# A fused attention and feed-forward kernel: another order of the opening on TensorE, and a later slot for one batch's projections

## The chip, the cores and the metric

The kernel runs on one core of a Trainium2 chip. The metric is the device time of one execution in microseconds. Five runs of the kernel before are shown, and one execution was profiled. Names of engines: PE is TensorE (matmuls), PEld its weight loads, DVE is VectorE, ACT is ScalarE, POOL is GpSimd, SP is SyncE. "L411" is line 411 of the kernel.

## What is computed

For 8 batches of 8 heads, with 1024 positions and 64 features per head, keys and values are first projected along the sequence to 64 rows (E and F), then a softmax attention is taken over these 64 rows, and the result goes through a feed-forward pair of matrices with a sigmoid-type GELU:

```python
k_proj = einsum('ks,bhsd->bhkd', E, k)            # 64 rows for each head
v_proj = einsum('ks,bhsd->bhkd', F, v)
scores = q @ k_proj.T / sqrt(64)
attn = softmax(scores)                            # over 64
x = (attn @ v_proj), heads side by side           # 8192 x 512
h = x @ w_in                                      # 8192 x 2048
out = (h * sigmoid(1.702 * h)) @ w_out            # 8192 x 512
```

Inputs and output are 32-bit floats; the kernel works in bfloat16 with 32-bit sums.

## The kernel before, in words

The 8192 tokens are cut into 16 blocks of 512 (two per batch). For each block j, `ffn1` (L405) makes 16 groups of 128 hidden features with four matmuls each, followed by a GELU on ACT; `ffn2` (L415) makes the four output tiles of 128 tokens, each out of 16 matmuls in two parts of eight. All else is put between these: a dictionary `fill` holds, for a block and a slot, the steps that are issued after that slot's matmuls (`at`, L446, and `filled`, L528). Slots 0 to 15 of a block follow one `ffn1` group each, slots O = 16 to 23 one part of `ffn2` each. The order of instructions on each engine is the order in which the program issues them; the tile library adds the waits.

For a batch b, `proj(b)` (L168) projects k and v (16 matmuls), `kv_out(b)` (L223) copies k's result on DVE, transposes it by a DMA from SP's queue into `kts`, and copies v's into `vqs`. `q_dma(b)` (L254) transposes q by a DMA, too. `scores(h, u)` (L274) is the score matmuls of half of the heads of block h, and their exp on ACT. `sums(h)` (L298) sums the exps of all heads in two `x_ps` tiles and takes reciprocals on DVE; `spread(h)` (L313) writes those to DRAM (`rdr`) and reads them back over the partitions (`rbc`), by DMAs from SP's queue. `values(h, u)` (L335) multiplies exps and projected v on PE, and DVE scales the two tiles by `rbc` (L341). Blocks 1 and 2 use `tok` and `x_tr` (L378, L393) for the same. PSUM is two pools of four buffers each: `f_ps` (L40), used by projections, scores, `ffn1` and `ffn2`, and `x_ps` (L41), used by sums, values, the transposes of x and some of the scores.

Loads go through POOL's queue in the order written at L88 to L105: k of batch 0 in three pieces, half of q, v in three pieces, w_in in eight pieces (two groups of hidden features each) with the other half of q among them, w_out in four, then batch 1. The buffers of k, v and q are single (q has two), so that a later load waits for the projection or transpose that reads the batch in them; `load(b)` for b from 2 on is issued at the start of block 2(b - 2).

The opening is block 0, written out by hand at L453 to L481. `k_piece` (L185) projects a piece of k and transposes it on PE. `q_tr0(g, u, cp)` (L234) makes eight transposes of q (half g of the block's tokens, half u of the heads) into an `f_ps` tile and copies it with the engine `cp`. `scores(0, u, half)` then works on 256 tokens. `sums0(half)` (L351) sums exps for 256 tokens with narrow matmuls, `v_piece` (L205) projects a piece of v, `tok0(p)` (L360) makes the values of a pair of heads and scales them on DVE in two instructions, and `x_tr0` (L370) transposes the result into x on PE and copies it. `warm(n)` (L140) is n matmuls on zeros whose result nobody reads. `gelu_table()` loads ACT's table.

Of the kernel before, what the change touches and what calls it, by code (L numbers as in the profile page):

```python
# [10 lines left out]
BF16 = mybir.dt.bfloat16  # L11
# [6 lines left out]
def kernel(ctx, tc, q, k, v, E, F,  # L18
                                                     moe_w_in, moe_w_out, out):
    nc = tc.nc  # L20
# [3 lines left out]
    P = 128  # L24
# [5 lines left out]
    TB = 512  # L30
    JB = TB // P
# [9 lines left out]
    ps_x = ctx.enter_context(tc.tile_pool(name="ps_x", bufs=4, space=PSUM))  # L41
# [50 lines left out]
    ident = consts.tile([P, P], BF16)  # L92
# [9 lines left out]
    for i in range(4):  # L102
        sl = slice(i * FC // 4, (i + 1) * FC // 4)
# [33 lines left out]
    def f_tile(shape, dt=F32):  # L137
        return ps_f.tile(shape, dt, name="f_ps")

    def warm(n, f=False):  # L140
        w_ps = f_tile([P, TB]) if f else ps_x.tile([P, TB], F32, name="x_ps")
        for _ in range(n):
            nc.tensor.matmul(w_ps, zeros[:, :P], zeros, start=True, stop=True)  # L143
# [18 lines left out]
    def eft(j, cols=slice(0, 2 * KP)):  # L162
        return efts[j // (J // 2)][:, j % (J // 2), cols]
# [4 lines left out]
    def proj(b):  # L168
        def go():
            kvps[b] = f_tile([P, H, D])  # L170
            for j in range(J):
                for e, r in enumerate((LO, HI)):
                    nc.tensor.matmul(kvps[b][r], eft(j, slice(e * KP, (e + 1) * KP)),  # L173
                                     (kt, vt)[e][b][:, :, j, :],
                                     start=(j == 0), stop=(j == J - 1))
        return go
# [8 lines left out]
    def k_piece(h0, n):  # L185
        k_ps = proj0(0, h0, n)
        k_b = att.tile([KP, n, D], BF16, name=f"k0_b{h0}", bufs=1)
        nc.vector.tensor_copy(k_b, k_ps[LO])
        warm(2)
        k_tr(k_b, h0 // 2)  # L190
# [14 lines left out]
    def v_piece(h0, n):  # L205

        v_ps = proj0(1, h0, n)
        if n == 4:
            nc.vector.tensor_tensor(vx0[0][:, :, :D], v_ps, mask, op=ALU.mult)
        else:  # L210
            for t in range(n):
                nc.scalar.activation(vx_of(0, h0 // 2)[:, t, :D], v_ps[:, t, :], AF.Identity,
                                     scale=rows[:, h0 % 4 + t:h0 % 4 + t + 1])

    def v_out(b, v_ps):
        vv = v_ps[HI].rearrange("k (u x) d -> k u x d", x=4)
        for r, xs_ in ((LO, X_LO), (HI, X_HI)):
            if b == 1:
                vx = vx1[r, :, :D].rearrange("k (u x) d -> k u x d", x=4)
                nc.vector.tensor_copy(vx[:, :, xs_], vv[:, :, xs_])  # L220
            nc.vector.tensor_copy(vqs[b % 2][r].rearrange("k (u e) d -> k u e d", e=2), vv[:, :, xs_, :])

    def kv_out(b):  # L223
        def go():
            ps = kvps.pop(b)
            k_b = att.tile([KP, H, D], BF16, name="k_b")
            nc.vector.tensor_copy(k_b, ps[LO])  # L227
            nc.sync.dma_start_transpose(out=kts[b % 2], in_=k_b.rearrange("k h d -> k (h d)"))
            v_out(b, ps)
        return go  # L230
# [3 lines left out]
    def q_tr0(g, u, cp):  # L234
        t_ps = f_tile([P, 2, 2, P], BF16)
        for jj in range(2):
            for h in range(4):
                r = h % 2 * D
                nc.tensor.transpose(t_ps[r:r + D, jj, h // 2, :], qt[0][:, 4 * u + h, 2 * g + jj, :], ident)
        cp(q0s[g][u], t_ps)  # L240
# [33 lines left out]
    def scores(h, u, half=None, x=False):  # L274
        b, c = divmod(h, NB2)
        j0, n = (c * JB, JB) if half is None else (c * JB + half * JB // 2, JB // 2)
        ts = slice(j0 * P - c * TB, (j0 + n) * P - c * TB)

        def go():
            if h not in expT:  # L280
                expT[h] = att.tile([P, HP, TB], BF16, name="expT", bufs=3)
            s_ps = [(x_tile() if x else f_tile([P, TB]))[:, :n * P] for _ in range(2)]
            eight(s_ps, [kts[b % 2][:, 2 * u + i, :] for i in range(2)],
                 [q0s[half][u][:, :, i, :] if h == 0 else qT[b][:, j0:j0 + n, 2 * u + i, :]
                   for i in range(2)])
            for i in range(2):
                nc.scalar.activation(expT[h][:, 2 * u + i, ts], s_ps[i], AF.Exp, scale=scale)  # L287
        return go

    def gelu_table():  # L290
        nc.scalar.preload_act_table(AF.Gelu_apprx_sigmoid)  # L291

    def x_of(h):
        if h not in xT:
            xT[h] = att.tile([P, KC, TB], BF16, name="xT", bufs=3)
        return xT[h]

    def sums(h):  # L298


        def go():
            d_ps = [ps_x.tile([P, TB], F32, name="x_ps") for _ in range(2)]
            for p in range(HP):
                for e in range(2):
                    r = HI if (p + e) % 2 else LO
                    nc.tensor.matmul(d_ps[e][32 * p:32 * p + 32], ones[r, :32], expT[h][r, p, :], start=True, stop=True)  # L306
            rden = att.tile([P, 2, TB], F32, name="rden", bufs=1)
            for e in range(2):
                nc.vector.reciprocal(rden[:, e, :], d_ps[e])  # L309
            rdens[h] = rden  # L310
        return go

    def spread(h):  # L313
        def go():
            rdr = dram.tile([HP, 2, TB], F32, name="rdr")
            nc.sync.dma_start(out=rdr, in_=rdens.pop(h)[0:P:32])
            rbc[h] = att.tile([P, HP, TB], F32, name="rbc")
            for e, r in enumerate((LO, HI)):
                nc.sync.dma_start(out=rbc[h][r], in_=rdr[None, :, e, :].to_broadcast([D, HP, TB]))
        return go  # L320
# [25 lines left out]
    xs = {}  # L346
# [4 lines left out]
    def sums0(half):  # L351
        d_ps = ps_x.tile([P, HP, 2, 2], F32, name="x_ps")
        for p in range(HP):
            for i in range(2):
                t = 2 * half + i
                nc.tensor.matmul(d_ps[:, p, i, :], expT[0][:, p, t * P:(t + 1) * P],
                                 vx_of(0, p)[:, :, D:].rearrange("r t o -> r (t o)"), start=True, stop=True)
        nc.vector.reciprocal(rd0[:, half], d_ps)

    def tok0(p):  # L360
        n_ps = ps_x.tile([P, 2, 2, 2, D], F32, name="x_ps")
        for t in range(JB):
            nc.tensor.matmul(n_ps[:, t // 2, t % 2].rearrange("s t d -> s (t d)"),
                             expT[0][:, p, t * P:(t + 1) * P], vx_of(0, p)[:, :, :D], start=True, stop=True)
        xs[p] = work.tile([P, 2, 2, 2, D], BF16, name="x0_sb", bufs=4)
        for a in range(2):
            nc.vector.tensor_tensor(xs[p][:, a], n_ps[:, a], rd0[:, a, p, :, :, None].to_broadcast([P, 2, 2, D]),
                                    op=ALU.mult)

    def x_tr0(p, parts, cp):  # L370
        n_ps = ps_x.tile([P, JB, P], BF16, name="x_ps")
        for g in range(parts):
            for t in range(g * JB // parts, (g + 1) * JB // parts):
                nc.tensor.transpose(n_ps[:, t, :], xs[p][:, t // 2, t % 2].rearrange("s t d -> s (t d)"), ident)  # L374
            sl = slice(g * JB // parts, (g + 1) * JB // parts)
            cp(x_of(0)[:, p, sl.start * P:sl.stop * P], n_ps[:, sl].rearrange("r t s -> r (t s)"))

    def tok(h, p, half):  # L378
        def go():
# [66 lines left out]
    def at(j, slot, *fs):  # L446
        fill.setdefault((j, slot), []).extend(fs)
# [5 lines left out]
    for h0, n in ((0, 4), (4, 2), (6, 2)):  # L453
        k_piece(h0, n)
    DV, AC = nc.vector.tensor_copy, nc.scalar.copy
    for half in range(2):
        q_tr0(half, 0, DV)
        q_tr0(half, 1, AC)
        for u in range(2):
            scores(0, u, half, u > 0)()  # L460
    warm(1)
    sums0(0)
    gelu_table()
    warm(1, True)
    v_piece(0, 4)
    sums0(1)
    v_piece(4, 2)
# [2 lines left out]
    warm(1, True)  # L470
    v_piece(6, 2)
    tok0(2)
    x_tr0(0, 1, AC)
    warm(1, True)
    x_tr0(1, 1, AC)
    tok0(3)
    warm(1, True)
    x_tr0(2, 1, AC)
    warm(1, True)
    x_tr0(3, 2, DV)  # L480
    warm(1, True)  # L481
    at(0, 13, q_tr(2))
    at(0, 15, q_tr(3))
    for u in range(2):
# [15 lines left out]
        at(1, O + 6, scores(3, u, None, u > 0))  # L500
    at(1, O + 6, gelu_table)
    at(1, O + 4, q_dma(2))
    at(2, 1, proj(2), kv_out(2), sums(3), spread(3))
    at(2, O, q_dma(3))
    at(2, O + 3, scores(5, 0))
    at(2, O + 6, proj(3), kv_out(3), scores(5, 1), sums(4), spread(4))
# [25 lines left out]
    for j in range(NBLK):  # L532
# [5 lines left out]
        parts = [(n, range(8 * g, 8 * g + 8)) for n in range(JB) for g in range(2)]  # L538
# [36 lines left out]
```

## Time and profile before

| | us |
|---|---|
| five runs | 510.13, 509.69, 513.47, 512.19, 512.19 |
| median of the runs | 512.19 |
| profiled execution, its own time | 510.13 |
| profiled execution, span from first to last instruction | 508.4 |
| PE busy in it | 499.8 |
| q's transposes begin on PE | 13.76 |
| ffn1 of block 0 begins on PE | 23.14 |
| proj(2) begins on PE | 89.11 |
| sums(4) begins on PE | 119.19 |

Times in the profile count from the first instruction. A row of the timeline has the start, the length, the engine, the line, the operation, what it writes and reads, the shapes, how many instructions of the kind follow one another, and in brackets the idle time of that engine before, with what ended it. Matmuls follow one another before the earlier ones have ended, so a row's length is a little more than the time to the next row's start. A row with SPq or POOL is the issue of a DMA; the data land later.

### The profile page before, as it was taken

The numbers are of one execution on the slowest core, as the hardware profiler recorded it, in microseconds if no ns is written. First come the engines' busy times: TensorE is split into PE (matmuls) and PEld (weight loads), VectorE is DVE, ScalarE is ACT, GpSimd is POOL, SyncE is SP. The second block draws the span as 40 slices with busy tenths as digits, with TensorE's granted clock in tenths as the row PEclk, the third lists the DMA queues.
The fourth block names the chain that finished last, engine by engine and source line by source line (L and its number), as shares of the span: only waits on it lengthen the run. The fifth ranks groups of instructions, "written<-read, shape, count | busy, mean of one in ns | idle before, by whom it ended". The sixth has DMA issues, their size and how long they took to land.

```text
span 508.4 us, 7125 instructions
## 1 busy us (share of the span) xinstructions
PE 499.8 (98%) x3049; PEld 226.9 (45%) x3049; DVE 154.7 (30%) x206; ACT 262.6 (52%) x429; POOL 77.2 (15%) x96
## 2 busy tenths in 40 slices
PE   7899999999999999999999999999999999999997
PEld 3644445444444444444444444444444444444444
DVE  4413204607251624216161330616223161611000
ACT  1665473655637365572746537374563737243351
POOL 7442150510600510051000510000000000000000
PEclk9999999999999999999999999999999999999999
DMA  9999999999899999598939969090703205050202
GB/s 165 200 203 207 215 152 173 202 207 139 159 208 256 118 183 185 159 141 93 221 58 209 122 112 229 26 226 0 173 0 83 86 17 151 0 168 0 84 0 84
DMA packets 124696, 68.77 MB, mean 135 GB/s; under 512 B 90564, under 2 KB 115524, under 8 KB 122744
## 3 DMA queue, kind: packets, MB, share of 16 engines
q0 software_dynamic: 83360, 29.37, 53.9%
q1 hardware_dynamic: 41224, 38.69, 30.6%
q8 instruction: 24, 0.39, 0.3%
q10 hardware_dynamic: 80, 0.26, 0.2%
q14 instruction: 8, 0.07, 0.0%
HBM read 72.88 MB, written 16.99 MB: 177 GB/s over the span
## 4 chain that ended last, share of the span: by engine, by line
PE 96%; DMA 2%; POOL 1%; ACT 1%; issue 0%; DVE 0%; POOLq 0%
PE f_ps L411 44%; PE f_ps L435 43%; PE f_ps L173 3%; DMA q_even<-in_q_dram 2%; PE f_ps L268 2%; PE x_ps L268 1%; PE f_ps L427 1%; PE x_ps L306 1%; POOL k_sb L57 0%; PE x_ps L383 0%; PE f_ps L181 0%; PE x_ps L398 0%; PE f_ps L143 0%; ACT expT L287 0%; PE f_ps L250 0%; PE x_ps L374 0%
## 5 line engine op out<-in xcount | busy, mean ns | idle before, releaser
L435 PE MATMUL f_ps<-w_out_sb,gT 128*128 128x512 bf16 x1008 | 226.7, 379 | 0.0
L411 PE MATMUL f_ps<-xT,w_in_sb 128*128 128x512 bf16 (+1 forms) x1032 | 224.3, 377 | 0.0
L413 ACT ACTIVATE gT<-f_ps 128x512 bf16<-128x512 f32 (+1 forms) x258 | 150.5, 594 | 61.9 <-PE f_ps L411 61.7
L411 PEld LDWEIGHTS <-w_in_sb 128*128 128x128 bf16 x1032 | 100.6, 98 | 119.8 <-issue 0.6
L435 PEld LDWEIGHTS <-gT 128*128 128x128 bf16 x1008 | 95.8, 98 | 121.8 <-issue 11.8
L438 ACT COPY o_sb<-f_ps 128x512 f32<-128x512 f32 x63 | 37.0, 587 | 130.7 <-PE f_ps L435 120.9
L341 DVE TENSOR_TENSOR xT<-x_ps,rbc 128x512 bf16<-128x512 f32 x52 | 33.4, 685 | 219.6 <-PE x_ps L268 117.0
L309 DVE RECIPROCAL rden<-x_ps 128x512 f32<-128x512 f32 x26 | 85.3, 3323 | 9.6 <-PE x_ps L306 9.6
L70 POOL DMA_DIRECT2D q_sb<-in_q_dram x48 | 42.1, 901 | 154.7 <-DMA qT<-q_sb 125.6
L287 ACT ACTIVATE expT<-f_ps 128x512 bf16<-128x512 f32 (+1 forms) x54 | 28.5, 580 | 29.4 <-PE f_ps L268 29.3
L287 ACT ACT_TABLE_LOAD x13 | 16.7, 1283 | 4.7 <-PE f_ps L268 4.5
L291 ACT ACT_TABLE_LOAD x14 | 18.0, 1283 | 0.2
L57 POOL DMA_DIRECT2D k_sb<-in_k_dram x10 | 8.5, 848 | 47.6 <-PE f_ps L173 44.7
L227 DVE CAST k_b<-f_ps 64x512 bf16<-64x512 f32 x7 | 4.8, 681 | 33.2 <-PE f_ps L173 33.2
L173 PE MATMUL f_ps<-k_sb,eft 128*64 128x512 bf16 x56 | 13.4, 382 | 0.0
L173 PE MATMUL f_ps<-v_sb,eft 128*64 128x512 bf16 x56 | 13.4, 382 | 0.0
L429 DVE COPY o_sb<-f_ps 128x256 f32<-128x256 f32 (+1 forms) x2 | 0.7, 358 | 37.3 <-issue 36.9
L268 PE MATMUL x_ps<-expT,vq 64*32 64x512 bf16 x208 | 10.2, 378 | 0.0
L268 PE MATMUL f_ps<-qT,kt 64*32 64x512 bf16 x200 | 10.2, 386 | 0.0
L57 POOL DMA_DIRECT2D v_sb<-in_v_dram x10 | 8.3, 838 | 7.8 <-DMA q_sb<-in_q_dram 4.1
L173 PEld LDWEIGHTS <-eft 128*64 128x64 bf16 x112 | 5.7, 109 | 7.3 <-issue 3.0
L268 PEld LDWEIGHTS <-kt 64*32 64x32 bf16 x272 | 3.6, 89 | 11.8 <-issue 11.1
(75 smaller groups left out, 129.9 us busy)
## 6 DMA issues: line engine op xcount, KB each, us to landing
out_dram<-o_sb SPq DMA_DIRECT2D x15, 1024.0 KB
rbc<-rdr SPq DMA_DIRECT2D x26, 512.0 KB
k_sb<-in_k_dram POOLq DMA_DIRECT2D x7, 1024.0 KB, 13.8
v_sb<-in_v_dram POOLq DMA_DIRECT2D x7, 1024.0 KB, 19.5
q_sb<-in_q_dram POOLq DMA_DIRECT2D x48, 128.0 KB, 7.7
w_in_sb<-in_moe_w_in_dram POOLq DMA_DIRECT2D x8, 256.0 KB, 12.2
w_out_sb<-in_moe_w_out_dram POOLq DMA_DIRECT2D x4, 512.0 KB, 14.8
q_even<-in_q_dram POOLq DMA_DIRECT2D x2, 512.0 KB, 10.7
```

Source lines behind the costliest of these rows:

```text
L57: nc.gpsimd.dma_start(out=dst[b][:, h:h + n, js:js + jn], in_=sv[:, h:h + n, js:js + jn])
L70: nc.gpsimd.dma_start(out=qt[b][:, j], in_=qv[:, j])
L173: nc.tensor.matmul(kvps[b][r], eft(j, slice(e * KP, (e + 1) * KP)), (kt, vt)[e][b][:, :, j, :], start=(j == 0), stop=(j == J - 1))
L268: nc.tensor.matmul(outs[i][r.start + c:r.start + c + 32], lhsTs[i][ri, c:c + 32], rhss[i][ri], start=True, stop=True)
L287: nc.scalar.activation(expT[h][:, 2 * u + i, ts], s_ps[i], AF.Exp, scale=scale)
L291: nc.scalar.preload_act_table(AF.Gelu_apprx_sigmoid)
L309: nc.vector.reciprocal(rden[:, e, :], d_ps[e])
L341: nc.vector.tensor_tensor(x_of(h)[:, 2 * u + i, :], n_ps[i], rbc[h][:, 2 * u + i, :], op=ALU.mult)
L411: nc.tensor.matmul(h_ps, w_in_sb[:, kc, fc * P:(fc + 1) * P], xT[j][:, kc, ts], start=(kc == 0), stop=(kc == KC - 1))
L413: nc.scalar.activation(gts[j][:, fc, ts], h_ps, AF.Gelu_apprx_sigmoid)
L435: nc.tensor.matmul(o_ps[n], gts[j][:, fc, n * P:(n + 1) * P], w_out_sb[:, fc, :], start=(fc == 0), stop=(fc == FC - 1))
L438: nc.scalar.copy(osb[j][:, n, :], o_ps.pop(n))
```

## The change

Three places change, all else stays.

- In the opening, four warm-up matmuls come right before q's transposes. All four groups of q's transposes are issued first (the copies of the second half both on DVE, those of the first on DVE and ACT), then the scores of both halves, then ACT's table load, the first sums, and v's projections. Two single warm-up matmuls around the first sums go.
- `x_tr0` takes the range of 256-token parts to do, and a tile for each call. The last pair of heads is done in two calls with a tile each, the first copied by ACT and the second by DVE, with a warm-up matmul between them; before, one call did two parts in one tile, both copied by DVE. One warm-up matmul goes here.
- In block 2, `proj(2), kv_out(2), sums(3), spread(3)` move from slot 1 to slot 3.

```diff
-    def x_tr0(p, parts, cp):
-        n_ps = ps_x.tile([P, JB, P], BF16, name="x_ps")
-        for g in range(parts):
-            for t in range(g * JB // parts, (g + 1) * JB // parts):
-                nc.tensor.transpose(n_ps[:, t, :], xs[p][:, t // 2, t % 2].rearrange("s t d -> s (t d)"), ident)
-            sl = slice(g * JB // parts, (g + 1) * JB // parts)
-            cp(x_of(0)[:, p, sl.start * P:sl.stop * P], n_ps[:, sl].rearrange("r t s -> r (t s)"))
+    def x_tr0(p, a, n, cp):
+        n_ps = ps_x.tile([P, 2 * n, P], BF16, name="x_ps")
+        for t in range(2 * n):
+            nc.tensor.transpose(n_ps[:, t, :], xs[p][:, a + t // 2, t % 2].rearrange("s t d -> s (t d)"), ident)
+        cp(x_of(0)[:, p, a * TB // 2:(a + n) * TB // 2], n_ps.rearrange("r t s -> r (t s)"))
...
     DV, AC = nc.vector.tensor_copy, nc.scalar.copy
+    warm(4)
     for half in range(2):
         q_tr0(half, 0, DV)
-        q_tr0(half, 1, AC)
+        q_tr0(half, 1, DV if half else AC)
+    for half in range(2):
         for u in range(2):
             scores(0, u, half, u > 0)()
-    warm(1)
+    gelu_table()
     sums0(0)
-    gelu_table()
-    warm(1, True)
     v_piece(0, 4)
     sums0(1)
     v_piece(4, 2)
...
     tok0(2)
-    x_tr0(0, 1, AC)
+    x_tr0(0, 0, 2, AC)
     warm(1, True)
-    x_tr0(1, 1, AC)
+    x_tr0(1, 0, 2, AC)
     tok0(3)
     warm(1, True)
-    x_tr0(2, 1, AC)
+    x_tr0(2, 0, 2, AC)
+    x_tr0(3, 0, 1, AC)
     warm(1, True)
-    x_tr0(3, 2, DV)
-    warm(1, True)
+    x_tr0(3, 1, 1, DV)
...
-    at(2, 1, proj(2), kv_out(2), sums(3), spread(3))
+    at(2, 3, proj(2), kv_out(2), sums(3), spread(3))
```

## The prediction

> **What bounds the kernel now.** I read the page's head first, then the chain of work that ended last and the waits of PE, and last the timeline of the two places that the change touches. The head and the waits of PE (engine and line, what it waited for, us in total, times, longest):
>
> ```profile
> span 508.4 us, 7125 instructions
> PE 499.8 (98%) x3049; PEld 226.9 (45%) x3049; DVE 154.7 (30%) x206; ACT 262.6 (52%) x429; POOL 77.2 (15%) x96
> ...
> PE f_ps L239 <- DMA q_even<-in_q_dram: 1.2, 1, 1.2
> PE f_ps L153 <- ACT ef_sb L147: 1.2, 1, 1.2
> ...
> PE x_ps L374 <- DVE xT L376: 0.4, 1, 0.4
> PE f_ps L268 <- ACT expT L287: 0.3, 1, 0.3
> PE f_ps L268 <- DVE q0T L240: 0.3, 1, 0.3
> PE x_ps L268 <- ACT q0T L240: 0.2, 1, 0.2
> ```
>
> PE is busy for 98% and after 23.14 us no wait of it is listed: the end is PE's work plus the opening. So time can be won only by work or waits that leave PE before 23.14, and lost wherever PE gets a wait that it does not have now. The opening in the timeline (start, length, engine, line):
>
> ```profile
> 13.76 0.64 PE L239 MATMUL f_ps<-ident,q_even 128*64 128x128 bf16 x16 [1.18 <-DMA q_even<-in_q_dram]
> 14.69 0.30 PE L268 MATMUL f_ps<-q0T,kt 64*32 64x256 bf16 x8 [0.30 <-DVE q0T L240]
> ...
> 16.77 0.30 PE L268 MATMUL x_ps<-q0T,kt 64*32 64x256 bf16 x8 [0.23 <-ACT q0T L240]
> 17.01 0.39 PE L143 MATMUL x_ps<-zeros 128*128 128x512 bf16 x1
> ...
> 19.88 0.61 PE L181 MATMUL f_ps<-v_sb,ffs 128*128 128x128 bf16 x8
> ...
> 22.81 0.27 PE L374 MATMUL x_ps<-ident,x_sb 128*128 128x128 bf16 x2 [0.38 <-DVE xT L376]
> 22.92 0.38 PE L143 MATMUL f_ps<-zeros 128*128 128x512 bf16 x1
> ```
>
> The reader should see the small waits between q's transposes (L239), scores (L268) and x's transposes (L374), and the warm-up matmuls (L143), each 0.22 us of PE (the next row starts so much later). The place of block 2, on PE, DVE and SP:
>
> ```profile
> 119.19 0.40 PE L306 MATMUL x_ps<-expT,ones 64*32 64x512 bf16 x8
> ...
> 117.44 2.48 DVE L341 TENSOR_TENSOR xT<-x_ps,rbc 128x512 bf16<-128x512 f32 x4 [18.16 <-DMA rbc<-rdr]
> ...
> 91.81 2.14 SPq L228 DMA_TRANSPOSE kt<-k_b  x1
> 99.31 0.62 SPq L316 DMA_DIRECT2D rdr<-rden  x1
> 105.01 1.32 SPq L319 DMA_DIRECT2D rbc<-rdr  x2
> ```
>
> DVE stands still for 18.16 us until the spread reciprocals (rbc) of block 3 land, and the four multiplies that follow free the four x_ps buffers. sums(4) at 119.19 needs two of them. They are free after two multiplies of 0.62, at 117.44 + 1.29 = 118.73 with the last one's tail: PE has 0.4 us to spare here, though no row calls it a wait.
>
> **The change, part by part.** All times are of the profiled execution: span 508.4, its own time 510.13. The median of the five runs is 512.19, 2.06 above.
>
> *Opening.* q's load lands as before, so the first transpose stays at 13.76. The new four warm-up matmuls (0.86) run from 12.58, where PE now waits until 13.76: they cost nothing, and would cost what q lands earlier than 13.45. All 32 transposes run at once (0.57 per 16): 14.90. Copies: DVE starts 0.16 after its group, 0.42 each, 0.35 apart: 14.63, 15.19, 15.54; ACT keeps one of its two (14.44 to 15.03). f_ps has four buffers and all hold q tiles, so the scores that follow get theirs as the copies end: second tile of half 0 at 15.03, of half 1 at 15.54. Four score groups of 0.24 then end at about 15.95 (before 17.07). The eight exps on ACT, 0.27 apart from 15.16, end at 17.4 instead of 17.84, since ACT has lost a 0.49 step in their midst. sums0(0) needs the first four: 16.35, a new wait of 0.4. v's pieces land at 16.3, 17.6 and 18.9 (issued at 4.98, 5.73 and 6.42; 11.3, 11.9 and about 12.4 to landing), now close to where PE wants them: v_piece(0,4) 16.6 to 17.45; sums0(1) waits for the last exp, 17.65; v_piece(4,2) to 18.12; two tok0 (0.23 each) and a warm-up to 18.8; v_piece(6,2) waits for its load at 18.9 and ends at 19.36 (before 20.35). Then DVE's eight multiplies, 0.35 each (19.64 to 22.42 before), run from 18.5 to 21.4 with a short wait for the last tok0. ACT copies x after v's last piece, from 20.03: three of 0.57 and the new half piece of 0.33, to 22.05. The last pair's transposes no longer stop for one another's copy (0.38). ffn1's first group needs that half piece last: it ends at 22.2, as if begun at 21.8; before, 23.14. Gain 1.35. It can't be less than the three warm-ups that go (0.65) unless a load is late, nor more than these and all four waits (0.30 + 0.30 + 0.23 + 0.38): 1.85. I take 1.35, the value worked out link by link. What is late next in the opening is ACT's x copies, then v's last load. w_in and w_out: ffn1 uses piece 0 at 21.8, which was issued at 7.12 and landed 13.0 later, at 20.1; the later pieces are used 1.73 apart and issued 1.3 to 2.6 apart. I cost them at nothing; if that cover fails, the whole 1.35 goes.
>
> *Clock.* From 12.6 to 17.0 PE was busy for 2.34 of 4.40 us, all transposes and narrow scores, and v's projection after it still ran at 0.87 per eight, 109 ns a matmul of 256 columns, half of what ffn1 takes for 512 (24 in 5.18: 216 ns). So that stretch cost no clock, and the new one (13.5 to 16.6) is shorter: nothing. [...]
>
> *Projections of batch 2, two slots later.* The same 1.85 us of PE and 0.34 of sums(3); nothing is added. Two ffn1 groups of 0.865 now come first. ffn1's four groups find f_ps buffers: two score tiles were freed by 86.6, one is spare, the output tile by ACT at 89.47, all 0.4 or more before they are wanted: nothing. v of batch 2 lands at 76.50 + 11.5 = 88.0 and was used at 89.11, 1.1 to spare; used 1.35 earlier it would have been a wait of 0.2, and the two slots take that away. Behind the moved group, everything shifts by 1.73 - 1.35 = +0.38: on DVE the k cast, two v copies and two reciprocals (6.57 together), on SP k's transpose, rdr and rbc, on POOL the loads of batch 3, which wait for proj(2) (k_sb at 91.32, v_sb, eight q_sb). Against PE, which is 1.35 earlier, rbc is 1.73 later.
>
> *The price of that at sums(4).* PE would be there at 119.19 - 1.35 = 117.84, the buffers at 118.73 + x, with x the shift of rbc's landing. Bounds of x: +0.38 if all keeps its distance from proj(2); -1.35 if it follows the transfers ahead of it, which come earlier with PE. From 87 to 95.2 the SP queue moved 2.08 MB (q's transposes and the output) and the loads 0.07 MB; only then did the new loads move. Those transfers hang on earlier PE work and loads and come about 0.9 earlier, the issues 0.38 later. I take the middle between 0.38 and -0.9, about -0.2, as both hold rbc. Wait: 1.35 - 0.4 - 0.2 = 0.75 us, between 0 and 1.33. What stays is 0.4 - x = 0.6, whatever the opening brought above that.
>
> Sum: -1.35 + 0.75 = -0.6. 510.13 - 0.6 = 509.5 for an execution like the profiled one, 512.19 - 0.6 = 511.6 for the median. I forecast 511.6; the ends are 0 and -1.85, so 510.3 to 512.2.
>
> **The rivals.**
> - *The gain is kept, and late loads hurt less.* Where v of batch 2 comes later than in this trace, before waits at proj(2) and after does not: up to 1.73 more. The runs lie in two groups (509.69, 510.13; 512.19, 512.19, 513.47), which fits some such stall of 2 us, but the trace shows none. Time: 512.19 - 1.35 = 510.8, with the stall gone as well 509.1; after runs of the lower group 509.9 - 1.35 = 508.5.
> - *The opening does not move.* If v's last load or ACT's copies hold ffn1 where it was, nothing is won, and the move alone takes 1.73 from the 0.4 to spare at sums(4): a wait of up to 1.3, so 512.2 to 513.5. For it: three of PE's new starts lie within 0.1 us of a landing. Against: q, v and w_in issues wait for nothing that the change moves.
> - *Slower: rbc falls into the q load.* From 108.5 to 114 the SP queue moved 488 packets, 89 per us; from 114 to 117.4, with the small packets of q of batch 3, 56, or 16 per us. If rbc starts so that 60 more of its packets fall into the second stretch, it lands 3 us later and sums(4) waits 3 us more: 512.19 - 0.6 + 3 = 514.6. It decides from x = 0.4, where the gain is gone, and counts as slower from x = 3. Against: the same small packets come 0.38 later too, and the 56 may only be the tail.
>
> **How the numbers follow.** Half a per cent is 2.56 us, about what a measurement of this kernel can tell from no change. Forecast 0.46, kept gain 0.28, no move 0.12, slower 0.14. Over 0.5% faster means under 509.6: most of the kept-gain case in lower-group runs or without the stall (0.20), and the forecast where after's median falls into the lower group (0.06): 0.26. Over 0.5% slower: 0.11 of the rbc case and 0.02 of no move. Within: 0.61. The range runs from 508.4 (lower group with the gain kept) to 513.6 (the highest run before, with the rbc case just begun); what is left out is the stronger half of the rbc case and a little below.
>
> **What would show it.** Right: the 0.30, 0.30 and 0.23 waits at L268 shrink to waits at the new sums and projections; x's last transposes have no 0.38 wait; ffn1 starts near 21.8; proj(2) starts near 89.5 with no wait; sums(4) has a PE wait on DVE's multiplies, and from there PE is about 0.6 ahead of before, to the end. Wrong: ffn1 at 22.8 or later (the opening), slow matmuls after 16.6 (the clock), no wait at sums(4) (x near -0.9 or below: gain 1.35), or one over 1.4 (rbc delayed by other loads).

## The result, and the profile after

The changed kernel takes 509.42 us (median of 30 runs, 508.83 to 511.12), the kernel before 511.04 (51 runs, 509.45 to 513.66). The ratio is 0.9969, with a 95% interval of 0.9960 to 0.9979: 1.6 us faster. The two ends tell more than the medians: the fastest run gained 0.6, the slowest 2.5. Of before's runs 31 of 51 lie above 510.5, of after's 2 of 30. So a good part of the gain is not a shorter program, but that long executions of it have become rare; the experiments ask what made them long.

The profiled execution after has a span of 507.5 (508.4 before) and an own time of 509.25. Its head and all waits of PE:

```profile
span 507.5 us, 7127 instructions
PE 501.5 (99%) x3050; PEld 227.4 (45%) x3050; DVE 155.1 (31%) x206; ACT 262.3 (52%) x429; POOL 77.2 (15%) x96
...
PE x_ps L143 <- DVE zeros L114: 1.2, 1, 1.2
PE f_ps L181 <- DMA v_sb<-in_v_dram: 1.1, 1, 1.1
PE f_ps L239 <- DMA q_even<-in_q_dram: 0.2, 1, 0.2
PE x_ps L356 <- ACT expT L287: 0.2, 1, 0.2
```

The waits between q's transposes, scores and x's transposes are gone, and so is the 1.2 for q, whose place the warm-up matmuls took. New are 0.2 at the first sums, and 1.1 for the last piece of v. The opening in PE's timeline of after:

```profile
13.40 1.08 PE L239 MATMUL f_ps<-ident,q_even 128*64 128x128 bf16 x32 [0.22 <-DMA q_even<-in_q_dram]
...
15.76 0.48 PE L356 MATMUL x_ps<-vx,expT 128*128 128x2 bf16 x8 [0.17 <-ACT expT L287]
16.11 1.03 PE L181 MATMUL f_ps<-v_sb,ffs 128*128 128x256 bf16 x8
...
19.66 0.61 PE L181 MATMUL f_ps<-v_sb,ffs 128*128 128x128 bf16 x8 [1.09 <-DMA v_sb<-in_v_dram]
...
22.24 0.28 PE L373 MATMUL x_ps<-ident,x_sb 128*128 128x128 bf16 x2
```

ffn1 begins at 22.35 (23.14 before). Of these 0.79, 0.36 are chance: q landed that much earlier here (its transposes begin at 13.40, not 13.76; over all profiles of this study between 13.03 and 14.08). From q's first transpose to ffn1 it is 8.95 instead of 9.38: the opening itself has won 0.43. The chain of work that ended last now leads back from v's last piece to its load:

```profile
6.41 13.21 DMA v_sb<-in_v_dram
19.62 0.04 issue
19.66 0.61 PE f_ps L181 x8
...
21.42 0.44 DVE x_sb L367
...
22.52 10.46 PE f_ps L409 x56
```

In block 2 the multiplies that free sums(4)'s buffers begin at 116.23 (117.44 before), and PE reaches sums(4) at 118.49 without a wait (timeline of DVE, then of PE, after):

```profile
116.23 2.48 DVE L341 TENSOR_TENSOR xT<-x_ps,rbc 128x512 bf16<-128x512 f32 x4 [15.92 <-DMA rbc<-rdr]
...
118.49 0.40 PE L306 MATMUL x_ps<-expT,ones 64*32 64x512 bf16 x8
```

### The profile page after: what moved, and what is told of

Read it like the earlier page. It is cut to its first block, busy times and chain, and to the rows that moved or that the text cites. A ratio compares the mean times of both kernels' runs of the same rounds, so it can differ in the third digit from the quotient of the medians.

```text
span 507.5 us, 7127 instructions
## 1 busy us (share of the span) xinstructions
PE 501.5 (99%) x3050; PEld 227.4 (45%) x3050; DVE 155.1 (31%) x206; ACT 262.3 (52%) x429; POOL 77.2 (15%) x96
## 4 chain that ended last, share of the span: by engine, by line
PE 95%; DMA 3%; POOL 1%; issue 0%; DVE 0%; ACT 0%; POOLq 0%
PE f_ps L409 44%; PE f_ps L433 43%; DMA v_sb<-in_v_dram 3%; PE f_ps L173 3%; PE f_ps L268 2%; PE x_ps L268 1%; PE f_ps L425 1%; PE x_ps L306 1%; POOL k_sb L57 0%; PE x_ps L381 0%; PE x_ps L396 0%; POOL v_sb L57 0%; PE f_ps L250 0%; POOL q_even L57 0%; PE x_ps L373 0%
## 5 line engine op out<-in xcount | busy, mean ns | idle before, releaser
L341 DVE TENSOR_TENSOR xT<-x_ps,rbc 128x512 bf16<-128x512 f32 x52 | 33.3, 685 | 217.4 <-PE x_ps L268 119.3
L143 PE MATMUL x_ps<-zeros 128*128 128x512 bf16 x26 | 9.2, 496 | 1.2 <-DVE zeros L114 1.2
## 6 DMA issues: line engine op xcount, KB each, us to landing
rbc<-rdr SPq DMA_DIRECT2D x26, 512.0 KB
w_out_sb<-in_moe_w_out_dram POOLq DMA_DIRECT2D x4, 512.0 KB, 14.7
q_even<-in_q_dram POOLq DMA_DIRECT2D x2, 512.0 KB, 11.0
```

The lines of the kernel that those rows point to most:

```text
L341: nc.vector.tensor_tensor(x_of(h)[:, 2 * u + i, :], n_ps[i], rbc[h][:, 2 * u + i, :], op=ALU.mult)
```

## The experiments

For each profile two lengths are given that separate the places, from q's first transpose to ffn1's start (the opening) and from ffn1's start to PE's last sums (where proj(2) and sums(4) lie), and the granted clock. Before: 9.38, 413.2, clock full. After: 8.95, 413.3, full. For the other runs the mean granted clock over the span is on record: 0.997 in the profiled run that was at half clock for 3.4 us, 0.993 in the one that was for 6.8 (both below); a run at 0.999 or 1.00 is called one at full clock here.

### The kernel before, a second profile

Unchanged.

> The kernel before, unchanged, for a second profile beside the first. Theory A (PE waits for v of batch 2 in most runs): if this execution is over 511, PE's waits list proj(2) at L173 with 0.5 to 3 us, behind a load of v that lands after 89; if it is under 510, none. Theory B (the runs differ in the opening): a run over 511 has its 1 to 3 us before 24 us, as longer waits for q, k or v's pieces. Theory C (rbc at sums(4)): a run over 511 has the wait at L306 near 119, behind DVE's multiplies. Time: 509.5 to 513.5, ratio 1.000.

Median 510.85 (509.53 to 512.21, 12 runs), ratio 1.0002 (0.9984 to 1.0019). The profiled execution took 511.57, and what it lost against the first one was lost before ffn1: q landed 0.32 later, and from q to ffn1 it took 10.53, 1.15 more; then it took 413.2 as before. No wait in the opening was longer. The windows of this profile show what it was (window, its length, busy time and instructions of PE, PEld, DVE, ACT, POOL, then the granted clock, DMA share, GB/s):

```profile
core 0: us, PE busy (x) PEld busy (x) DVE busy (x) ACT busy (x) POOL busy (x), PEclk, DMA share, GB/s
12.90:16.40 3.50, 1.81 (x48) 1.26 (x48) 0.93 (x3) 1.64 (x5) 0.74 (x1) 1.00 1.24 205
16.40:19.80 3.40, 3.12 (x33) 1.69 (x34) 0.37 (x2) 3.11 (x7) 1.97 (x3) 0.50 1.38 200
19.80:24.60 4.80, 4.37 (x63) 3.64 (x63) 3.67 (x12) 2.63 (x7) 2.64 (x4) 1.00 1.46 195
```

After 3.5 us in which PE was busy for 1.81, with nothing but q's transposes and the narrow score matmuls, the clock was granted at 0.50 for 3.4 us, and then in full again. In its timeline v's first piece shows it, 1.5 us for what took 0.87 in the first profile:

```profile
18.48 1.69 PE L181 MATMUL f_ps<-v_sb,ffs 128*128 128x256 bf16 x8
20.01 0.35 PE L356 MATMUL x_ps<-vx,expT 128*128 128x2 bf16 x8
```

Theory B (the opening) holds as to the place, but not by longer waits for loads; A (proj(2) waits for v) and C (sums(4)) fall for this execution.

How often that happens, the granted clock of the other runs tells. Of the 120 executions of the kernel before that were timed in this study beside the variants (these 12 among them), 42 had a mean clock of 0.997 or less, and their median is 512.0; the other 78, at full clock, have 510.1. So the lost clock is there in about a third of the runs. It is not the whole of the spread: of the 66 runs above 510.5, 25 were at full clock, and none of those was profiled.

### The four warm-up matmuls alone

```diff
     DV, AC = nc.vector.tensor_copy, nc.scalar.copy
+    warm(4)
     for half in range(2):
```

> The kernel before with nothing but the four warm-up matmuls ahead of q's transposes. Clock theory (r1's granted clock was 0.50 from 16.4 to 19.8, and its ffn1 began 1.5 late): with PE kept at work until q lands, no run loses the clock; the runs above 510.5 go, median 509.6 to 509.9, lowest still 509.4, PEclk 1.00 from 13 to 24. Rival (the slow runs come from late loads): median 510.7 and spread of 3 us stay. My prediction's reading (the clock is no matter): no difference from before, ratio 1.000.

Median 509.66 (509.23 to 510.51, 11 runs), ratio 0.9979 (0.9965 to 0.9993); the opening took 9.38, exactly what the first profile of before took. So 0.86 us of matmuls on zeros, put into a wait, did not change the length of an opening that kept the clock. None of the 11 runs lost the clock, and of the 28 runs of before on the same chip 8 did. The clock theory's numbers are met, my reading (no difference) is not. The median fell by 1.05; that this is all the clock is not shown, as the 20 runs of before at full clock have a median of 510.35, still 0.7 above these. At proj(2) this profile has the short wait for v that the opening alone has (0.3, below), and from ffn1 to the last sums it took 413.5.

### The whole change without them

```diff
     DV, AC = nc.vector.tensor_copy, nc.scalar.copy
-    warm(4)
     for half in range(2):
```

> The whole change without the four warm-up matmuls. Clock theory: the stretch without dense matmuls is then 12.4 to about 16.1, a little shorter than before's 12.4 to 17.0, so some of the runs lose the clock: lowest 508.8 as with them, but a part of the runs 1 to 2.5 above, median 509.4 to 510.5 and spread over 2 us. Rival (the new order alone does it): median 509.2 to 509.4, narrow, the same as the whole change.

Median 509.44 (508.21 to 510.69, 11 runs), ratio 0.9980 (0.9966 to 0.9994): 1.27 below before's median on that chip and 0.23 above the whole change's (below). Six of the 11 runs lie more than 1 us above the fastest; of the whole change's 11 none does. That is the spread that the clock theory expected, but not its cause: all 11 runs were at full clock, the six long ones too, and the profiled one took 8.64 from q to ffn1. So the new order without the warm-up matmuls lost the clock in none of 11 runs either, as my prediction had it for its shorter stretch; 11 runs are few for that. What spreads these runs stays open. That the warm-up matmuls are needed in the whole change is not shown.

### More PE instructions early on

```diff
     warm(12)
+    w_ps = ps_x.tile([P, TB], F32, name="x_ps")
+    for _ in range(20):
+        nc.tensor.matmul(w_ps[:, :P], zeros[:, :P], zeros[:, :P], start=True, stop=True)
```

> The kernel before with 20 narrow matmuls (128 columns) on zeros right after the first twelve, where PE waits for E and F: some 40 PE instructions more, 1.1 us of idle time filled. Late-piece theory: PE's instruction load (queue q8) comes 0.7 to 1.7 earlier than in before, where it came at 19.0, so it falls before v's last piece has landed, and that lands more than 1.8 after the piece before it (1.25 before). Rival (the late piece has to do with the new order or ACT's table load): q8 may move, and the pieces still land 1.25 apart. Time within 1 us of before.

One run, 512.24, 1.5 above before's median and not within 1 as expected: this execution was at half clock for 6.8 us on end, twice as long as the second profile of before, and its opening took 11.96 (windows of this run):

```profile
12.90:15.65 2.75, 1.80 (x48) 1.26 (x48) 0.60 (x2) 1.49 (x5) 0.74 (x1) 1.00 1.24 205
15.65:22.40 6.75, 6.12 (x65) 4.49 (x65) 2.18 (x8) 3.78 (x10) 3.12 (x4) 0.50 1.38 199
```

What it was made for came out too. A 16 KB load of the kind "instruction" (queue q8, 24 of them over the span; I take them for PE's, as this one moved with PE's instructions) came at 17.17 instead of 18.99, and v's last piece landed 2.26 after the one before (17.34 and 19.60), not 1.25. POOL's issues, which wait for v's three pieces one after another, show it. First the kernel before:

```profile
16.55 0.74 POOL L86 DMA_DIRECT2D w_in_sb<-in_moe_w_in_dram  x1 [1.81 <-DMA v_sb<-in_v_dram]
17.89 0.89 POOL L57 DMA_DIRECT2D q_even<-in_q_dram  x1 [0.60 <-DMA v_sb<-in_v_dram]
19.14 0.75 POOL L86 DMA_DIRECT2D w_in_sb<-in_moe_w_in_dram  x1 [0.36 <-DMA v_sb<-in_v_dram]
```

Then this run:

```profile
16.26 0.74 POOL L86 DMA_DIRECT2D w_in_sb<-in_moe_w_in_dram  x1 [1.80 <-DMA v_sb<-in_v_dram]
17.62 0.89 POOL L57 DMA_DIRECT2D q_even<-in_q_dram  x1 [0.62 <-DMA v_sb<-in_v_dram]
19.89 0.75 POOL L86 DMA_DIRECT2D w_in_sb<-in_moe_w_in_dram  x1 [1.38 <-DMA v_sb<-in_v_dram]
```

Such a piece lands in 16 shares: in after 15 of the last piece's had landed by 18.50 and the last came at 19.62, in before all 16 by 18.86. The order of the opening and ACT's table load were those of before here, so the late piece is not theirs.

### The opening alone

```diff
-    at(2, 3, proj(2), kv_out(2), sums(3), spread(3))
+    at(2, 1, proj(2), kv_out(2), sums(3), spread(3))
```

(against the whole change)

> The new opening and the two tiles for x's last transposes, with the projections of batch 2 left in slot 1. Theory A: the opening brings 0.7 to 1.3 to ffn1's start, and v of batch 2 is then waited for in nearly every run: the median stays within 0.5 of before (510.5 to 511.5), and the runs spread as widely as before, with a wait at L173 of 0.3 to 2 us. Theory B: median 509.4 and narrow, like the whole change, with no wait after 23. My prediction's sum without its give-back: 1.35 less than before, 509.7.

Median 509.24 (508.70 to 509.82, 12 runs), ratio 0.9968 (0.9954 to 0.9981): all of the gain, and narrow. Theory B's number. At proj(2) the trace has a short wait, 0.3 us between k's first matmul and v's:

```profile
88.32 0.40 PE L173 MATMUL f_ps<-k_sb,eft 128*64 128x512 bf16 x1
88.65 0.38 PE L173 MATMUL f_ps<-v_sb,eft 128*64 128x512 bf16 x1
```

v of batch 2 landed at 88.6. From ffn1 to the last sums it took 413.6, 0.4 more than before.

### The later slot alone

```diff
-    at(2, 1, proj(2), kv_out(2), sums(3), spread(3))
+    at(2, 3, proj(2), kv_out(2), sums(3), spread(3))
```

(against the kernel before)

> The opening of before, with the projections of batch 2 in slot 3. Theory A: the slow runs go; median 509.6 to 510.2, spread of the runs about 2 us, no wait at L173. Theory B: median and spread as before, 511.0. My prediction's price at sums(4) (rbc 1.73 later against 0.4 to spare): 1.3 us slower than before, 512.3, with a wait at L306.

Median 510.08 (509.45 to 513.35, 12 runs), ratio 1.0002 (0.9983 to 1.0022): the median lies 0.64 below before's on that chip, but the mean is the same and the ratio shows no gain; the wide spread of before is there (5 of the 12 runs had a mean clock of 0.992 to 0.997), so A falls. In the profile (full clock, opening 9.38) the multiplies began at 117.91, and PE stood at sums(4):

```profile
118.65 0.37 PE L306 MATMUL x_ps<-expT,ones 64*32 64x512 bf16 x1
119.25 0.41 PE L306 MATMUL x_ps<-expT,ones 64*32 64x512 bf16 x7 [0.23 <-DVE xT L341]
```

From ffn1 to the last sums it took 414.0, 0.8 more than before. The price at sums(4) is there, at 0.8 and not at the 1.3 of my sum, in one execution; the timing can't tell 0.8 from nothing.

### The later slot, later still

```diff
-    at(2, 3, proj(2), kv_out(2), sums(3), spread(3))
+    at(2, 5, proj(2), kv_out(2), sums(3), spread(3))
```

> The whole change with batch 2's projections, sums(3) and spread(3) in slot 5 instead of 3. Margin theory (rbc's landing follows the move, PE's way to sums(4) gets 1.73 shorter; sums(4) had 0 to 1 us to spare with slot 3): PE waits 0.7 to 1.7 us at sums(4), L306, for DVE's multiplies at L341, which begin 1.5 to 2 later than with slot 3, near 118.5; median 1 to 1.5 above the whole change, 510.2 to 510.9. Rival (rbc's landing is set by the loads in the DMA queues and not by when it is issued, as in the first profile after, where it came earlier although it was issued later): no wait, median 509.3.

Median 510.37 (509.85 to 511.19, 10 runs), 1.0 to 1.2 above the whole change's two medians, the second of them from another chip; against before on its own chip the ratio is 0.9998 (0.9984 to 1.0012), so that the gain is gone. PE's timeline has this wait:

```profile
118.89 0.37 PE L306 MATMUL x_ps<-expT,ones 64*32 64x512 bf16 x1 [0.38 <-DVE xT L341]
119.48 0.41 PE L306 MATMUL x_ps<-expT,ones 64*32 64x512 bf16 x7 [0.23 <-DVE xT L341]
```

The multiplies began at 118.14, and from ffn1 to the last sums it took 414.5, 1.2 more than after. So the mechanism holds: rbc does come later with the move, and sums(4) pays. With slot 3 the whole change stands near the edge of it: in its first profile the multiplies began 2.26 before sums(4), without a wait, in its second (below) 1.20 before, with a short one.

### The whole change once more

Unchanged.

> The whole change once more, on the same chip as the others, for a second profile: median 509.3, spread 1 to 2 us. Late-piece theory: v's last piece lands more than 2.0 after the one before it, since PE's instruction load falls between them, and PE waits 0.8 to 1.3 for it. If the wait in the first profile was chance: the pieces land 1.3 apart and the wait is under 0.4, ffn1 at 21.9. Give-back at sums(4): a wait there in this profile only if DVE's multiplies begin after 117.1.

Median 509.21 (508.85 to 509.71, 11 runs), ratio 0.9967 (0.9953 to 0.9981). v's last piece landed 2.3 after the one before again (17.20 and 19.52; q8 at 17.18), PE waited 1.26 for it, and the opening took 8.89. The multiplies began at 117.20, and eight sums at 118.40 took 0.55 instead of 0.40: a give-back of 0.15.

### The two tiles alone, and the order without them

```diff
+    x_tr0(3, 0, 1, AC)
     warm(1, True)
-    x_tr0(3, 2, DV)
-    warm(1, True)
+    x_tr0(3, 1, 1, DV)
```

(against the kernel before, with `x_tr0` of the change)

> The kernel before with only the last pair's transposes in two tiles, the first copied by ACT, and one warm-up matmul less. All theories: ffn1 starts 0.2 to 0.6 earlier, as the 0.38 wait and 0.22 of warm-up go. Theory A: the gain is lost in most runs at proj(2), median within 0.3 of before. Theory B: 0.4 faster.

Median 509.88 (509.04 to 511.89, 12 runs), ratio 0.9989 (0.9971 to 1.0007). The opening took 8.83 at full clock: 0.55 less. The runs spread as widely as before, and 6 of the 12 had a mean clock of 0.993 or 0.997; these have neither the four warm-up matmuls nor the new order.

The reverse, the change's opening (its order and four warm-up matmuls) with `x_tr0` as before and slot 1:

```diff
-    x_tr0(3, 0, 1, AC)
     warm(1, True)
-    x_tr0(3, 1, 1, DV)
+    x_tr0(3, 2, DV)
+    warm(1, True)
```

> The new order of the opening with its four warm-up matmuls, but x's last transposes in one tile as before and the projections of batch 2 in slot 1. If v's last piece, which lands late, sets the opening's end: the 0.38 wait of x's last transposes is still on the path, so ffn1 begins 0.4 to 0.6 later than with the two tiles, near 22.8, and the median is 509.5 to 509.8 (opening with two tiles 509.24). If the tiles do nothing here: 509.2.

Median 509.68 (509.37 to 510.17, 12 runs), ratio 0.9981 (0.9968 to 0.9994); v's last piece was late (1.25 of wait), the wait of 0.38 at x's last transposes was there, and ffn1 began at 22.81: 9.43 after q, as long as before. Next to the four warm-up matmuls the new order of transposes and scores has won nothing; what it wins in front of v's last piece, it waits for that piece. The tiles bring 0.44 between the medians (509.68 and 509.24).

### Fewer warm-up matmuls

```diff
-    warm(4)
-
     def eft(j, cols=slice(0, 2 * KP)):
...
         nc.vector.tensor_copy(k_b, k_ps[LO])
-        warm(2)
         k_tr(k_b, h0 // 2)
```

> The whole change without the four warm-up matmuls after E's transposes and the three pairs in k's pieces: 20 PE instructions fewer ahead of v's pieces. Late-piece theory: PE's instruction load comes 0.5 or more later, at 17.7 to 18.2, mostly behind v's last piece, which then lands 1.3 to 1.8 after the one before; PE's wait for it falls from 1.1 - 1.3 to 0.3 - 0.8 and the fastest run is 508.3. Clock theory: E's transposes and k's pieces have less dense work, so some runs lose the clock there or later, and the runs spread over 2 us. Both may hold; the profile's clock and landings tell them apart.

Median 510.14 (508.31 to 512.14, 12 runs), ratio 0.9987 (0.9969 to 1.0005). The clock theory's part came true for some: 7 of 12 runs lie more than 1 us above the fastest, three of them with a mean clock of 0.990 to 0.995; the other four, the profiled one among them, were at full clock. The other part failed: q8 came at 17.90, 0.7 later as expected, but v's last piece landed at 19.93, and PE waited 1.7. In the four warm-ups alone, with a q8 load at 18.0, v's piece was in time (POOL waited 0.45 for it), but the load behind it, w_in's first piece, was not: POOL's issue that waits for it came 2.07 us after the one that waits for v's last piece, against 1.30 in the first profile of before. The later slot alone (2.06) and the two tiles (2.14) show the same. So with q8 at 18.0, too, a landing is late, one piece further on. In all four profiles with a load seen between 17.1 and 17.3 v's piece was late (last section); why it was late here at 17.90 and not there at 18.0 is open.

### Work put into the wait

```diff
     warm(1, True)
-    v_piece(6, 2)
     tok0(2)
     x_tr0(0, 0, 2, AC)
-    warm(1, True)
     x_tr0(1, 0, 2, AC)
-    tok0(3)
-    warm(1, True)
+    v_piece(6, 2)
     x_tr0(2, 0, 2, AC)
+    warm(1, True)
+    tok0(3)
     x_tr0(3, 0, 1, AC)
...
+        elif h0 == 6:
+            nc.vector.tensor_tensor(vx0[2][:, :, :D], v_ps, mask[:, 2:], op=ALU.mult)
...
-    at(2, 3, proj(2), kv_out(2), sums(3), spread(3))
+    at(2, 2, proj(2), kv_out(2), sums(3), spread(3))
```

> The whole change, with the third pair's values and the first two pairs' transposes put ahead of v's last piece, where PE waits 1.1 to 1.3 us, that piece masked by one instruction on DVE instead of two on ACT, and batch 2's projections in slot 2. If the chain from v's last landing to ffn1 sets the opening (v_piece 0.6, ACT 0.53, tok0 0.4, DVE 0.42, transpose 0.25, ACT 0.33): PE's wait for v falls to 0.3 to 0.7, ffn1 begins 0.3 to 0.6 earlier, near 21.9; median 508.7 to 509.0, against 509.2 to 509.4 of the whole change. If what is won is lost at sums(4) or proj(2): a wait of 0.2 to 0.6 at L306 or L173 and median 509.3.

Median 509.12 (508.66 to 510.64, 12 runs), ratio 0.9973 (0.9958 to 0.9988). The wait for v is gone, ffn1 began at 22.08 (8.71 after q, 0.2 less than after), and no wait came up at proj(2) or sums(4). Two new waits of PE took most of the place of the old one: 0.44 at the third pair's values (L365), for ACT, which masks the piece before, and 0.52 at the last pair's transposes (L375), for DVE. Its span, 507.2, is the shortest with the four warm-up matmuls. The gain is half or less of what was expected, and by the runs it can't be told from the whole change.

## Why the prediction was right or wrong

The forecast was 511.6 with a range of 508.4 to 513.6 and most of the chance within half a per cent. The time, 509.42, lies in the range and the change of 0.31% within that bound, but that is owed to the width of both and not to the sum: the gain was forecast at 0.6 and is 1.6, and 511.6 lies above even before's 511.04, since the median of the five runs that the forecast started from (512.19) was 1.15 too high. The way was wrong in three of its steps.

*Clock: put at nothing, and part of the gain.* I took one profile, in which the clock stayed full over 4.4 us of transposes and narrow scores, as proof that such a stretch costs nothing. It was one execution. The second profile of the same kernel lost the clock behind such a stretch, with 0.50 granted for 3.4 us, and took 1.15 us longer from q to ffn1, and 42 of 120 runs have a mean clock as low. Why one execution lost the clock and another of the same program kept it is not shown (last section). My argument that the new, shorter stretch costs nothing is not contradicted: without the warm-up matmuls it lost the clock in none of 11 runs. What I costed wrong is the kernel before, whose stretch did cost, and the four warm-up matmuls, which I put at nothing because they lie in a wait: alone they bring the median 1.05 down.

*Opening: 1.35 forecast, 0.43 and 0.49 measured from q on.* The links up to v's second piece held within 0.25 us, when counted from q's landing (sums0(0) 2.36 after q's first transpose, forecast 2.6; v's first piece 2.7, forecast 2.8). The step that failed is "v_piece(6,2) waits for its load at 18.9": it came at 19.66, or 6.26 after q's first transpose instead of 5.14. I had named v's last load as the next thing to be late, and then used its old landing time, as if an issue that hadn't moved made a landing that didn't move. The two tiles held: 0.38 of wait and a warm-up matmul, 0.55 by themselves.

*Give-back at sums(4): 0.75 forecast; 0, 0.15, and 0.8 and 1.2 where it was provoked.* (With the 0.46 to spare that its rows give, and not 0.4, the sum comes to 0.69.) The mechanism is right: the later slot alone and slot 5 both show PE waiting at L306 for L341. The size was off since x, the shift of rbc's landing, was -1.2 and -0.2 in the two profiles of after, where -0.2 was taken and -1.35 was the bound, and because PE came later than forecast, by what the opening did not win. The wait at proj(2) that the move was to spare, 0.2 by my sum, is 0.3 in the profiles of the opening alone and of the four warm-up matmuls alone, and none in the order without the tiles. As both are of a few tenths and of opposite sign, the move's sum is nothing that the runs can tell (509.24 without it, 509.21 and 509.42 with it).

*The rivals.* The kept gain came nearest in time, and the two groups of runs that I saw there were real; that their cause was a late v at proj(2) is refuted by the later slot alone, which kept the spread. The opening that does not move came half true: v's last load held it, and of the 1.35 only what the tiles bring was left. That rbc falls into q's load did not happen. The cover of w_in held: no wait at ffn1.

Together: on one chip the median fell by 1.05 with the four warm-up matmuls alone, by 1.27 with the rest of the change without them, and by 1.50 with all of it. The parts overlap, so they can't be added up: after the warm-up matmuls the rest brings 0.45 more, after the rest the warm-up matmuls 0.23. What is shown is that the tiles shorten the opening by 0.55 and the four warm-up matmuls all but end the runs that lose the clock (1 of 98 with them, 42 of 120 of before); next to these two, the new order and the later slot add nothing measurable. By itself the new order may end those runs, too (without the warm-up matmuls none of 11 lost the clock). Why runs at full clock still differ, by 2.5 us in the whole change without the warm-up matmuls, stays open.

## What to carry to other kernels

When runs of one program spread by more than the effect that is sought, one profile stands for one of several executions: look at where its time lies among the runs, and profile a second one before calling a cost nothing. Read the granted clock of each run, too: a spread like that of a lost clock came up here in runs that had all kept it. Here a stretch on PE made of transposes and narrow matmuls was followed by half clock in two profiled executions, with no wait over 1.2 us in it, and four matmuls on zeros (0.86 us), put into a wait that was there anyway, ended that (none of 11 runs lost the clock, against 8 of 28, and the opening still took 9.38). Before a step is moved up against a load, look at how evenly the load's 16 shares land, and what else is fetched at that time.

## What the runs showed of the hardware

- The granted clock fell to 0.50 for 3.4 us in one execution of the kernel before (16.4 to 19.8), and for 6.8 in one with 40 PE instructions more (from 15.65), after 2.75 to 3.5 us in which PE was busy for half to two thirds of the time (1.81 of 3.50 us, 1.80 of 2.75); in another execution of the kernel before it did not fall. In the runs of this study that have the four warm-up matmuls ahead of q's transposes and those in k's pieces the mean clock was below 0.999 in 1 of 98 runs (0.996).
- How busy PE was does not tell these executions apart: the clock stayed at 1.00 through and after 12.60 to 17.00 in the first profile of before (PE busy for 2.34 of 4.40 us, 53%) and 12.40 to 15.80 in the whole change without the four warm-up matmuls (2.11 of 3.40, 62%), and it fell after 52% and 65%. What decides it was not shown.
- A load of 16 KB of instructions (q8) came 1.8 us earlier with 40 PE instructions more ahead of it (17.17, not 18.99) and 0.6 to 0.7 later with 20 fewer (17.90); it is one packet, which took 0.89 us in before and 0.98 in after. Where it is seen between 17.1 and 17.3 us (after, its second profile, the opening alone, more PE instructions), with the DMA engines busy for 90% or more in every slice from 16.5 to 20, v's last 256 KB piece was late, in four profiles of four: POOL waited 1.38 to 1.51 us for it, against 0.36 and 0.38 in the two profiles of before, where the load came at 19.0. In after the last share landed 1.1 us after the other 15. That it is the load itself, and not something that goes with it, is argued from its time and size and from the run that moved it; it was not removed. PE's waits in before and after list none for instructions; another transfer seems to pay.
- rbc was issued between 105.0 and 107.1 in before, after, the later slot alone and slot 5, and the multiplies began 11.0 to 12.5 later: its issue sets the landing to within 1.5 us, which is more than sums(4) has to spare (0.46 in before).
